# A spectral gate kernel: filtering the frequency columns in two passes, upper half first

## The chip, the core and the metric

The kernel runs on one core of one Trainium2 chip. The metric is device time in microseconds (us), the median of a few executions. A second number is the span of one profiled execution, from the first to the last of the program's own instructions; positions in the text ("at 72.1 us") count from the start of that span.

The core has a matrix engine (TensorE, PE in the profile, with its weight loads as PEld), a vector engine (VectorE, DVE), an activation engine (ScalarE, ACT), a general engine (GpSimd, POOL) and a queue engine that only issues transfers (SyncE, SP). Each runs its own list of instructions in order; semaphores make one engine wait for another.

## The reference, cut to what matters

```python
x = A_x                                       # (1, 2048, 1024) bf16
g = sigmoid((x * gate_w).sum(-1, keepdims=True))
def branch(x, w_r, w_i):                      # w: (2048, 513) bf16
    X = rfft2(x.astype(float32))              # over the 2048 rows and the 1024 columns
    return irfft2(X * (w_r + 1j * w_i), s=(2048, 1024)).astype(bf16)
out = g * branch(x, A_w_r, A_w_i) + (1 - g) * branch(x, B_w_r, B_w_i)
```

One forward transform of x, two products with filters of 513 frequency columns, two inverse transforms, and a mix of both by a gate of one number per row.

## The kernel before, in words

All transforms are matrix products with constant tables. The text names the steps as the code does:

- **s1**: eight groups of rows are loaded (`load.x`), folded (`fold`), multiplied on PE (`s1m`) and copied from the accumulators to the array FR by ACT or DVE (`s1e`). Together the sixteen `s1e` fill sixteen blocks of 1024 elements per partition, t = 0 to 15. Every later step needs all sixteen.
- **s2 and s4**: for each t the transform along the columns (`s2m`, copied by `s2e`) and the rest of the transform along the rows (`s4m`, copied by `s4e`). A block then holds real and imaginary parts in alternate partitions.
- **swap**: two transfers inside the on-chip memory that exchange even and odd partitions, so that a complex product needs no other partition.
- **xneg**: a change of sign in every second partition (on DVE or ACT), after the swap has read the block.
- **prod**: the product with the filters, both branches at once, on DVE. `prod2` takes the swapped block, `prod1` the signed one, each for one half h of the 512 frequency columns (h = 0 lower, h = 1 upper), 1024 elements per partition. That is 16 x 2 x 2 = 64 instructions. The results go to the array WP.
- **s5, s6, s7**: the inverse transform. `s5m.g`, g = 0 to 31, handles 16 columns (16 PE products, then the copy `s5e.g` by ACT or DVE); groups 0 to 15 are the lower half and 16 to 31 the upper. `s6m.p.h` and `s7m.i` follow; `s7c` (ACT) and `s7p` (DVE) take out the accumulators, `fin` (POOL and DVE) forms the output rows, `store` writes them.
- **the gate**: `gwm`, `gsm`, `stm`, `rowsum`, `zsm`, `zse` compute it; `zst` and `zld` send it through main memory to broadcast it, `rb` and `al` put it into the table of s6.
- **filters**: `load.W.b.f` brings block b (two values of t) of branch f into one of three buffers (`WR`), as whole rows of 513 columns: pieces of 2052 bytes.

The accumulators are four units of 1024 columns. A unit is taken by the next PE step in order and given back by the copy that reads it. The order on every engine is written out by hand in one list, `ORDER`; each entry is a step, its numbers and the engine or queue (a, d, p, s) that takes it. An entry's place in the list fixes its place on its engine and nothing else; the waits follow from the tiles that a step reads and writes:

```python
for job in ORDER.split():
    P.job = job
    name, *args = job.split(".")
    jobs[name](*(int(k) if k.isdigit() else k for k in args))
```

All instructions of one kind are issued by a helper, so a line of the profile is a kind: L309 transfers, L313 copies by ACT, L315 copies by DVE and POOL, L318 products on DVE, L322 and L324 `xneg` on ACT and DVE, L333 PE, L718 `s7p`, L724 `fin`.

Of the kernel before, what the change touches and what calls it, by code (L numbers as in the profile page):

```python
# [24 lines left out]
fold.6.0.d fold.7.0.d load.F2.s s1m.1.0 s1e.5.1.a s1e.1.1.a s1m.6.1 s1m.6.0 s1m.7.0 load.W.1.0.s load.CK.s s1e.6.1.d s1e.1.0.a s1e.6.0.a
s1m.7.1 s1e.7.0.a fold.2.0.d fold.2.1.d s1e.7.1.a s1m.2.0 s1m.2.1 s1e.2.1.a load.W.0.1.s s1e.2.0.d s2m.0 sig0 s2m.1 load.W.0.0.s s2e.1.d
gsm.0.4 s2e.0.a s4m.0 s4e.0.a s2m.2 gse.0.4.d s4m.1 s2m.3 s2e.2.d s4m.2 load.W.1.1.s w5.0.a swap.0.a s4e.1.a s4e.2.a load.W.2.1.s s2e.3.d
s2m.4 s2e.4.a s4m.3 s2m.5 prod2.0.0.d swap.1.s s4m.4 swap.2.s xneg.0.d gsm.4.4 prod2.0.1.d s4e.3.a s2m.6 load.W.2.0.s prod1.0.1.d s2e.5.a
s4e.4.a s4m.5 s2m.7 s2e.6.a prod1.0.0.d s4m.6 s4e.5.a prod2.1.0.d xneg.1.d swap.3.p prod2.1.1.d prod1.1.0.d prod1.1.1.d s2m.9 swap.4.s
prod2.2.1.d w5.1.a s2e.7.a prod2.2.0.d prod2.3.1.d w5.2.a xneg.2.d s4e.6.a xneg.3.a prod2.3.0.d s4m.7 load.W.3.0.s gse.4.4.a prod2.4.1.d  # L30
s4e.7.a s2e.9.a prod2.4.0.d load.W.3.1.s prod1.2.0.d gsm.8.4 swap.5.p swap.6.p prod1.2.1.d s2m.8 swap.7.s prod1.3.1.d prod1.3.0.d xneg.4.d
s2m.11 s2e.8.a s4m.9 prod2.5.1.d xneg.5.d s4m.8 prod1.4.1.d gse.8.4.a xneg.6.d prod1.4.0.d s2m.10 load.W.4.0.s s2e.11.a s4e.9.a load.W.4.1.s
s2m.12 prod2.6.0.d gsm.12.4 s4e.8.a s4m.11 s2e.10.a swap.9.p prod1.5.1.d s4m.10 prod2.5.0.d gse.12.4.a prod1.5.0.d s2m.13 w5.3.a xneg.7.a
s4e.11.a s4e.10.a swap.8.p prod1.6.0.d s2e.13.a prod2.6.1.d prod2.7.1.d load.W.5.0.s s2m.15 prod1.6.1.d s2m.14 xneg.8.d prod2.8.0.d
prod1.7.0.d s4m.13 w5.4.a load.W.5.1.s s2e.12.a xneg.9.a load.VC.s swap.11.p s4m.12 prod2.9.1.d s4e.13.a prod2.7.0.d prod2.9.0.d s2e.14.a
prod2.8.1.d w5.5.a prod1.7.1.d s4e.12.a prod1.9.0.d s4m.14 prod2.11.1.d swap.10.s swap.13.s prod1.8.0.d s2e.15.a prod1.9.1.d prod1.8.1.d stm
s4e.14.a s4m.15 xneg.11.a s4e.15.a load.W.6.0.s load.W.6.1.s xneg.10.a rowsum.0.d load.W.7.0.s prod2.10.1.d load.W.7.1.s prod1.11.1.d
xneg.13.a prod1.11.0.d swap.12.p xneg.12.a prod1.10.0.d swap.14.p prod2.13.1.d prod1.10.1.d w5.6.a swap.15.p prod1.13.1.d prod2.12.1.d
rowsum.1.d prod1.12.1.d rowsum.2.p xneg.14.a prod2.14.1.d xneg.15.a prod1.14.1.d zsm prod2.15.1.d prod1.15.1.d s5m.16 prod2.10.0.d ste.a
prod1.14.0.d w5.7.a s5m.24 s5m.26 zse prod2.11.0.d prod2.14.0.d stx.s prod1.15.0.d prod1.13.0.d prod1.12.0.d s5m.22 load.U5.s prod2.12.0.d  # L40
s5e.16.a s5m.23 s5e.24.a prod2.15.0.d s5e.22.a s5m.29 s5e.29.a zst.p s5m.27 s5e.23.a s5e.26.d prod2.13.0.d s5m.19 s5e.27.a s5m.30 s5m.25
s5m.6 s5e.30.a s5e.19.d s5e.6.a s5m.18 stp.2.d s5e.25.d s5m.3 s5e.18.a s5m.13 s5m.28 s5e.3.d stp.1.d s5e.13.a stp.0.d s5m.8 s5e.28.a s5e.8.d
s5m.31 s5m.15 s5m.17 s5e.31.a s5m.14 s5e.15.d s5m.10 s5e.17.a s5e.14.d s5e.10.a s5m.2 zld.s c0m rb.0.d s5m.21 c0e.d al.0.1.d s5e.2.a s5m.12
al.0.0.d load.DI.s s5m.1 s5e.21.a s5m.11 s5m.7 s5e.12.d s5e.1.a s5m.20 s5m.9 s5e.11.d s5m.5 s5e.7.a s5e.20.d s5m.0 s5e.9.a s5e.0.a s5m.4
# [8 lines left out]
fin.10.1.p s7p.11.1.d s6m.7.1 store.6.0.s fin.10.0.d store.1.0.s s7p.12.0.d store.8.1.s s6e.7.0.a s7p.12.1.d store.4.1.s store.7.1.s
store.9.0.s s6e.7.1.a fin.12.1.d fin.11.1.p store.3.1.s s7m.13 fin.12.0.p s7m.14 store.10.0.s s7c.13.a s7m.15 store.9.1.a s7c.14.a
s7p.13.0.d fin.11.0.p s7p.13.1.d s7p.14.0.d store.8.0.s store.12.0.a s7p.14.1.d s7c.15.a store.12.1.s store.10.1.s fin.13.0.d store.11.0.s
s7p.15.0.d store.14.0.s fin.13.1.p store.14.1.a s7p.15.1.d store.13.1.s store.11.1.a store.15.1.a store.15.0.s store.13.0.p
# [14 lines left out]
def make_consts():  # L71
# [187 lines left out]
def bass_gated_mix__spectral_gfnet__spectral_gfnet__prompt_kernel(nc, A_x, A_w_r, A_w_i, B_x, B_w_r, B_w_i, gate_w, out):  # L259
# [29 lines left out]
    def ps(col, dims):  # L289
        return AP(PS, col, [[4096, 128]] + [list(x) for x in dims])  # L290
# [510 lines left out]
```

## Time and profile before

| | |
|---|---|
| time, median of 3 runs | 133.83 us (133.65 to 135.38) |
| the profiled execution's own time | 134.36 us |
| its span | 132.1 us |
| busy: PE, DVE, ACT, POOL | 102.8, 106.5, 98.5, 40.3 us |
| bytes moved | 25.54 MB in 15602 packets |

A group's row of the profile gives the line, the engine, the operation, the tile written and the tile read with partitions and elements, the count, the busy time, the mean length of one in ns, and the idle time in front of them with what ended it. A row of a stretch gives, for each engine, busy time and count of instructions, then the granted clock of PE (1.00 is full speed), the mean busy share of the 16 transfer engines and the bytes moved per second. A row of the timeline gives start, length, engine, line, tiles and count. PEld overlaps PE. "SPq" is SP issuing a transfer.

### The profile page before, as it was taken

To read this page: it belongs to the slowest core of one execution; us is meant where nothing else is said; L and a number is where in the kernel's file an instruction comes from. 1 tells how busy PE (TensorE), PEld (TensorE's weight loads), DVE (VectorE), ACT (ScalarE), POOL (GpSimd) and SP (SyncE) were. 2 spreads that over 40 slices of the span, in tenths; PEclk is the share of its full clock that TensorE was granted. 3 is DMA by queue.
4 is the path that set the end of the run, shared out by engine and by line. 5 is a ranking of instruction groups with operands and counts; after the bars stand their busy time and mean duration, and the time that the engine had idled before them with its cause. 6 is when DMAs were issued, how large, how long until landed. Compare 5 with 4: busy or idle time off the path is not lost.

```text
span 132.1 us, 3396 instructions
## 1 busy us (share of the span) xinstructions
PE 102.8 (78%) x1383; PEld 82.6 (63%) x1383; DVE 106.5 (81%) x162; ACT 98.5 (75%) x132; POOL 40.3 (30%) x47
## 2 busy tenths in 40 slices
PE   6169899699999999542001999999999999999900
PEld 3047788566866576120001988999999999978400
DVE  0325677268999989999489997999799999999980
ACT  1603999948999999989852679999957998787310
POOL 3000000000315063025111000000004999999990
PEclk9999999999999999997555569999999999999995
DMA  4899999903579887877960946200000021335565
GB/s 109 240 360 344 349 393 377 353 21 119 188 269 268 294 294 250 323 240 245 330 249 10 321 158 211 117 5 0 5 0 5 0 97 66 135 143 204 201 235 205
DMA packets 15602, 25.54 MB, mean 193 GB/s; under 512 B 2514, under 2 KB 7394, under 8 KB 15330
## 3 DMA queue, kind: packets, MB, share of 16 engines
q1 hardware_dynamic: 12288, 20.31, 45.7%
q10 hardware_dynamic: 2306, 2.37, 5.4%
q0 software_dynamic: 992, 2.63, 5.1%
q8 instruction: 11, 0.18, 0.6%
q14 instruction: 5, 0.04, 0.1%
HBM read 16.90 MB, written 4.20 MB: 160 GB/s over the span
## 4 chain that ended last, share of the span: by engine, by line
PE 45%; DVE 15%; DMA 13%; ACT 8%; issue 7%; POOL 7%; SPq 2%; POOLq 0%; DVEq 0%; ACTq 0%
PE PS L333 45%; DVE WP L318 11%; POOL WR L724 7%; DMA WR<-in_B_w_i_dram 5%; ACT FR L313 5%; DMA WP<-c_E 4%; DMA FR<-FR 4%; ACT WP L313 3%; SPq L309 2%; DVE FR L718 2%; DVE FR L315 1%; ACT W L313 0%; DVE F L318 0%; POOLq L740 0%; POOL FR L309 0%
## 5 line engine op out<-in xcount | busy, mean ns | idle before, releaser
L313 ACT ACTIVATE FR<-PS 128x1024 bf16<-128x1024 f32 (+1 forms) x57 | 49.2, 908 | 16.9 <-PE PS L333 14.4
L318 DVE TENSOR_TENSOR WP<-FR,WR 128x1024 bf16<-128x1024 bf16 x64 | 39.9, 687 | 2.9 <-DMA WR<-in_B_w_i_dram 2.1
L313 ACT ACTIVATE WP<-PS 128x1024 bf16<-128x1024 f32 x35 | 34.0, 1025 | 5.7 <-PE PS L333 5.5
L724 POOL TENSOR_TENSOR WR<-FR 128x512 bf16<-128x512 f32 x18 | 26.8, 1516 | 29.8 <-DVE FR L718 29.7
L333 PE MATMUL PS<-FR,WP 128*128 128x128 bf16 (+2 forms) x384 | 32.1, 245 | 0.3 <-DVE FR L718 0.2
L333 PEld LDWEIGHTS PS<-FR,WP 128*128 128x128 bf16 x384 | 28.0, 130 | 3.9 <-DVE FR L718 0.9
L333 PE MATMUL PS<-CK,WP 128*128 128x64 bf16 x512 | 20.4, 207 | 3.5 <-DVE WP L318 2.9
L309 POOL DMA_DIRECT2D FR<-FR x18 | 9.9, 552 | 42.0 <-DVE WP L318 23.0
L333 PEld LDWEIGHTS PS<-CK,WP 128*128 128x128 bf16 x512 | 19.8, 120 | 3.9 <-DVE WP L318 3.0
L333 PE MATMUL PS<-FR,CK 128*128 128x512 bf16 x64 | 16.2, 380 | 3.3 <-ACT FR L313 3.2
L333 PE MATMUL PS<-WP 128*128 128x256 bf16 (+1 forms) x128 | 14.8, 281 | 4.4 <-DMA WP<-in_A_x_dram 3.3
L718 DVE TENSOR_TENSOR FR<-PS,FR 128x512 f32<-128x512 f32 x28 | 17.7, 678 | 0.3
L315 DVE CAST WP<-PS 128x1024 bf16<-128x1024 f32 (+1 forms) x14 | 15.9, 1166 | 2.1 <-PE PS L333 1.8
L333 PE MATMUL PS<-F,FR 128*128 128x256 bf16 x128 | 16.0, 273 | 1.5 <-ACT FR L313 1.2
L333 PEld LDWEIGHTS PS<-WP 128*128 128x128 bf16 x128 | 11.7, 108 | 8.1 <-DMA WP<-in_A_x_dram 4.1
L333 PEld LDWEIGHTS PS<-F,FR 128*128 128x128 bf16 x128 | 12.0, 98 | 5.3 <-ACT FR L313 1.8
L315 DVE CAST FR<-PS 128x1024 bf16<-128x1024 f32 x7 | 8.6, 1224 | 6.6 <-PE PS L333 6.6
L322 ACT ACTIVATE FR<-FR,SM 128x1024 bf16<-128x1024 bf16 x9 | 10.3, 1154 | 2.0 <-DMA FR<-FR 2.0
L333 PEld LDWEIGHTS PS<-FR,CK 128*128 128x128 bf16 x64 | 5.6, 98 | 9.2 <-ACT FR L313 4.7
L724 DVE TENSOR_TENSOR WR<-FR 128x512 bf16<-128x512 f32 x10 | 9.8, 981 | 0.1
L333 PE MATMUL PS<-ATB,CK 128*64 128x32 bf16 x1 | 0.2, 234 | 8.7 <-POOL ATB L315 8.7
L324 DVE TENSOR_SCALAR WP<-WP,SM 128x1280 bf16<-128x1280 bf16 (+1 forms) x3 | 1.4, 507 | 6.3 <-DMA SM<-c_SM 3.6
(44 smaller groups left out, 46.4 us busy)
## 6 DMA issues: line engine op xcount, KB each, us to landing
out_dram<-WR SPq DMA_DIRECT2D x24, 128.0 KB, 2.1
WP<-in_A_x_dram SPq DMA_DIRECT2D x11, 256.0 KB, 7.8
FR<-FR POOLq DMA_DIRECT2D x18, 128.0 KB, 4.1
WR<-in_A_w_r_dram SPq DMA_DIRECT2D x7, 256.5 KB, 3.6
WR<-in_A_w_i_dram SPq DMA_DIRECT2D x7, 256.5 KB, 4.5
WR<-in_B_w_r_dram SPq DMA_DIRECT2D x7, 256.5 KB, 5.1
WR<-in_B_w_i_dram SPq DMA_DIRECT2D x7, 256.5 KB, 5.8
FR<-FR SPq DMA_DIRECT2D x12, 128.0 KB, 2.6
```

What stands on the lines that cost most here:

```text
L309: return P.add(eng, lambda e: e.dma_start(dst, src), dma=name, **kw)
L313: P.add("act", lambda e: e.activation(dst, src, ACT.Copy), **kw)
L315: P.add(eng, lambda e: e.tensor_copy(dst, src), **kw)
L318: P.add(eng, lambda e: e.tensor_tensor(out=dst, in0=s0, in1=s1, op=ALU.mult), **kw)
L322: P.add("act", lambda e: e.activation(dst, src, ACT.Copy, scale=SM[:, col:col + 1]), **kw)
L324: P.add(eng, lambda e: e.tensor_scalar(out=dst, in0=src, scalar1=SM[:, col:col + 1], scalar2=None, op0=ALU.mult), **kw)
L333: P.add("pe", lambda e: e.matmul(o, lh, rh, start=first, stop=last), **kw)
L718: P.add(Q[eng], lambda e: e.tensor_tensor(out=o, in0=ps(u * 1024, [(1, 512)]), in1=eos(i), op=ALU.subtract if s else ALU.add), r=[("EO", i ...
L724: P.add(Q[eng], lambda e: e.tensor_tensor(out=od, in0=pv[:, :, 0, :], in1=pv[:, :, 1, :], op=ALU.subtract if s else ALU.add), r=[("PQ", i ...
```

## The change

The 512 frequency columns are now handled in two passes, h = 1 first.

- `s2m.p.h`, `s4m.p.h`, `swap.p.h` and `xneg.p.h` handle two values of t (p = 0 to 7) for one half of the columns. The elements per step stay at 1024. The `s2m` products have 128 columns in place of 256 and there are twice as many (256 for 128). For p = 0 `s4m` is cut in two, since t = 0 has tables of its own.
- `prod.t.h` does in one instruction of 2048 elements what `prod2.t.h` and `prod1.t.h` did in two of 1024: 32 instructions for 64. It needs the swap and the sign change both.
- The upper half's blocks lie in WP, in room that x and the table E have left; the lower half's stay in FR. No product of h = 0 may write before everything of h = 1 has been read.
- `load.W.h.b.m.f` brings half rows: pieces of 514 bytes (h = 1) or 512 bytes (h = 0), four values of t per block. A transfer of four rows moves half the bytes that one of two whole rows moved, so there are 72 transfers for 36.
- `s5m` of groups 16 to 31 stands between the lower half's steps.
- The first warm-up on PE has 14 products of 512 columns in place of 4. `sig0`, which loads the table of the sigmoid, stands ahead of the first `s1e`. The first group of rows is 5 in place of 4; 13 `s1e` are on ACT in place of 12.
- At the end DVE has 13 `fin` in place of 10 and POOL 15 in place of 18; `rb.0`, `rb.3` and three of the `al` move to POOL. The gate is loaded into F2, and U5, DI and the buffers of s7 get other places in FR.

```diff
-load.x.0.1.s warm.12x64x1.4x512x1 load.x.5.0.a load.GR.a load.x.5.1.a fold.4.0.d fold.3.0.d s1m.4.0 s1m.4.1 s1m.3.1 load.x.1.0.s fold.0.0.d
+warm.12x64x1.14x512x1 fold.7.0.d load.x.0.0.s s1m.5.0 load.x.0.1.s fold.0.1.d load.x.3.0.s fold.0.0.d load.x.3.1.s load.x.6.0.s egen.0.1
...
         elif what == "W":
-            b, f = k
...
-                    s = AP(src.tensor, src.offset + 2 * b * 513, [[32 * 513, 64], [(31 - 4 * b) * 513, 2], [1, 1026]])
-                    dma(Q[q], f"w{b}{f}", sl(WR, d0, [(1026, 2), (1, 1026)], p0=ri, np_=64, pstep=2), s, **kw)
...
+            h, b, m, f = k
+            slot, n = (4 * (1 - h) + b) % 3, 256 + h
...
+                    dma(Q[q], f"w{h}{b}{f}", sl(WR, slot * WS + (4 * j + 2 * f + pm) * RW, [(4 * RW, c), (1, n)], p0=ri, np_=64, pstep=2),
+                        AP(src.tensor, src.offset + row * 513 + 256 * h, [[32 * 513, 64], [st, c], [1, n]]), **kw)
...
+    U = [("prod", 0)]
+    def place(kind, p, h):
+        if h:
+            return WP, 8192 * (3 - kind) % 24576 + 1024 * p, [("U", kind, p)]
+        v = 2 * p + (kind == 1)
+        return FR, v * 1024, UK(v * 1024)
...
-    def xneg(t, eng):
-        sign(Q[eng], sl(FR, t * 1024, [(1, 1024)]), sl(FR, t * 1024, [(1, 1024)]), 1, r=["SM"], w=[("FR", t), ("XN", t)])
+    def xneg(p, h, eng):
+        T, o, K = place(1, p, h)
+        sign(Q[eng], sl(T, o, [(1, 1024)]), sl(T, o, [(1, 1024)]), 1, r=["SM"], w=K + [("XN", p, h)])
...
-        i0 = sl(FR, slot * 1024 + 256 * h, [(0, 2), (512, 2), (4, 64), (1, 4)])
-        o = sl(WP, h * HZ + (256 if k == 1 else 0) + 16 * t, [(8, 2), (4, 2), (BP, 64), (1, 4)])
+        i0 = sl(T, y + 512 * (t % 2), [(x - y, 2), (0, 2), (1, 512)]).rearrange("p k f (m q l) -> p k f m q l", m=2, l=4)
+        i1 = sl(WR, slot * WS + 4 * RW * (t % 4), [(0, 2), (2 * RW, 2), (RW, 2), (4, 64), (1, 4)])
+        o = sl(WP, h * HZ + 32 * t, [(16, 2), (8, 2), (4, 2), (BP, 64), (1, 4)])
```

What moves, on three engines. First PE, where the last steps of s2 and s4 meet s5. `PS<-F,FR` is `s2m`, `PS<-FR,CK` is `s4m`, `PS<-CK,WP` is `s5m` (16 per group), `PS<-GSB,CK` is `stm`, `PS<-ATB,CK` is `zsm`. Before:

```order
L333 MATMUL PS<-F,FR 128x256 x24
L333 MATMUL PS<-FR,CK 128x512 x12
L333 MATMUL PS<-GSB,CK 128x15 x2
L333 MATMUL PS<-GSB,CK 128x1 x2
L333 MATMUL PS<-FR,CK 128x512 x4
L333 MATMUL PS<-ATB,CK 64x32
L333 MATMUL PS<-CK,WP 128x64 x352
```

And now, at the same place:

```order
L333 MATMUL PS<-F,FR 128x128 x16
L333 MATMUL PS<-CK,WP 128x64 x16
L333 MATMUL PS<-GSB,CK 128x15 x2
L333 MATMUL PS<-GSB,CK 128x1 x2
L333 MATMUL PS<-CK,WP 128x64 x16
L333 MATMUL PS<-ATB,CK 64x32
L333 MATMUL PS<-CK,WP 128x64 x16
L333 MATMUL PS<-FR,CK 128x512 x8
L333 MATMUL PS<-CK,WP 128x64 x304
```

All of s5 stood behind the last `s4m`; now three groups of the upper half stand ahead of the last two `s4m`, and the other groups follow, upper half first.

Second ACT, around the last sign changes. `FR<-PS` with 1024 elements are `s4e` and `s2e`, `FR<-FR,SM` is `xneg`, `W<-WR` is `w5`, `WP<-PS 128x8x128` is `s5e`, `ZG<-PS` is `zse`, `XST<-PS` is `ste`. Before:

```order
L322 ACTIVATE FR<-FR,SM 128x1024
L313 ACTIVATE FR<-PS 128x1024
L322 ACTIVATE FR<-FR,SM 128x1024 x3
L313 ACTIVATE W<-WR 128x4 x2
L322 ACTIVATE FR<-FR,SM 128x1024 x2
L313 ACTIVATE XST<-PS 128x32
L313 ACTIVATE W<-WR 128x4 x2
L628 ACTIVATE ZG<-PS 64x32 x2
L313 ACTIVATE WP<-PS 128x8x128 x21
```

And now:

```order
L313 ACTIVATE WP<-PS 128x8x128 x2
L632 ACTIVATE ZG<-PS 64x32 x2
L322 ACTIVATE FR<-FR,SM 128x1024
L313 ACTIVATE FR<-PS 128x2x2x256 x2
L313 ACTIVATE WP<-PS 128x8x128 x3
L313 ACTIVATE XST<-PS 128x32
L313 ACTIVATE WP<-PS 128x8x128 x3
L322 ACTIVATE FR<-FR,SM 128x1024
L313 ACTIVATE WP<-PS 128x8x128
L322 ACTIVATE FR<-FR,SM 128x1024 x2
L313 ACTIVATE WP<-PS 128x8x128 x16
```

The last two `s4e` and the last four `xneg` of the lower half on ACT now stand between nine copies of the upper half's s5; the other sixteen copies follow.

Third SP, where filters are loaded into a buffer that is in use. The bracket names the semaphores that the transfer waits for (`d_w..` an earlier load, `s_dve` and `s_act` the products and `w5` that read it). Before, two blocks in a row:

```order
L309 DMA WR<-in_A_w_r_dram 64x2x1026 [waits d_w10,s_dve]
L309 DMA WR<-in_A_w_i_dram 64x2x1026
L309 DMA WR<-in_B_w_r_dram 64x2x1026 [waits d_w11]
L309 DMA WR<-in_B_w_i_dram 64x2x1026
L309 DMA WR<-in_A_w_r_dram 64x2x1026 [waits d_w20,s_dve]
```

And now, the first five of the eight transfers of one block:

```order
L309 DMA WR<-in_A_w_r_dram 64x4x256 [waits d_w120,s_dve,s_act]
L309 DMA WR<-in_A_w_i_dram 64x4x256
L309 DMA WR<-in_A_w_r_dram 64x4x256
L309 DMA WR<-in_A_w_i_dram 64x4x256
L309 DMA WR<-in_B_w_r_dram 64x4x256 [waits d_w121]
```

A block was four transfers for two values of t; it is eight for four values of t and half the columns.

More of the change, by code (lines that the diff above doesn't have):

```diff
@@ L25 @@
[L25 to L44, printed above, removed]
@@ L53 @@
[L53 to L56, printed above, removed]
+load.E.1.s load.SM.a load.x.5.1.a egen.1.3 load.x.5.0.s fold.5.0.d zero load.E.0.s egen.1.1 load.GR.a load.x.7.0.a egen.1.2 load.x.7.1.s
@@ L57 @@
+store.11.0.s s7c.14.a s7p.13.1.d s7c.15.a s7p.14.0.d s7p.14.1.d s7p.15.0.d s7p.15.1.d store.14.0.a store.14.1.a store.15.1.a fin.13.0.d
+fin.13.1.d store.15.0.s store.12.0.a store.13.0.s store.13.1.a store.12.1.p
 """
@@ L408, in load @@
         elif what == "VC":
[L409 removed]
+            dma(Q[q], "VC", sl(WP, VCo, [(1, 512)]).bitcast(u16), cst["V"].ap(), w=["VC"] + [("fold", FOLDED[0], k) for k in range(2)])
         elif what == "GR":
```

217 lines of the change are left out of this document (116 added, 101 removed).

## The prediction

> **What bounds the kernel now.** First the page's slices, where PE has a hole; then stretches cut at its edges, to see who works in it; then the chain, to see whether it sets the end.
>
> ```profile
> PE   6169899699999999542001999999999999999900
> PEclk9999999999999999997555569999999999999995
> 24.30:55.00 30.70, 30.23 (x312) 20.52 (x312) 26.32 (x44) 27.70 (x42) 6.66 (x12) 1.00 0.67 228
> 55.00:72.10 17.10, 2.39 (x13) 1.00 (x14) 14.52 (x25) 12.77 (x21) 4.46 (x8) 0.68 0.68 232
> 72.10:93.20 21.10, 20.57 (x528) 20.20 (x529) 19.40 (x27) 18.49 (x20) 0.00 (x0) 0.86 0.38 128
> 93.20:125.70 32.50, 32.14 (x390) 28.04 (x387) 31.77 (x46) 24.85 (x35) 24.75 (x18) 1.00 0.24 86
> ...
> 57.04 3.10 DVE WP L318 x5
> ...
> 62.77 6.64 DMA WR<-in_B_w_i_dram
> ...
> 69.54 2.52 DVE WP L318 x4
> 72.06 0.05 issue
> 72.10 5.32 PE PS L333 x96
> 77.42 0.02 issue
> 77.45 3.78 ACT WP L313 x4
> 81.23 0.05 issue
> 81.28 30.36 PE PS L333 x596
> ```
>
> From 55.0 to 72.1 PE works 2.39 of 17.1 us, and the clock falls. The chain there is products on DVE and a filter block; at 72.1 the first s5 group starts, when the last product of the upper half is done. Then come 21.1 us of s5 alone, and from 93.2 PE is full to the end. Two stages stand one behind the other that need not, as far as data goes: the last products and the first sixteen groups of s5.
>
> **The change, term by term.** I follow three queues to the start of s6 (93.2 before) and add the rest.
>
> ```profile
> 15.00:20.00 5.00, 4.59 (x53) 3.79 (x52) 4.30 (x7) 4.67 (x7) 0.00 (x0) 1.00 1.07 381
> 8.17 7.34 PE L333 MATMUL PS<-WP 128*128 128x256 bf16 x47 [0.69 <-DVE WP L315]
> L333 PE MATMUL PS<-F,FR 128*128 128x256 bf16 x128 | 16.0, 273 | 1.5 <-ACT FR L313 1.2 <-ACT GSB L313 0.2
> 17.48 6.76 ACT L313 ACTIVATE FR<-PS 128x1024 bf16<-128x1024 f32 x7 [0.33 <-PE PS L333]
> 31.67 0.68 DVE L318 TENSOR_TENSOR WP<-FR,WR 128x1024 bf16<-128x1024 bf16 x1
> FR<-FR SPq DMA_DIRECT2D x12, 128.0 KB, 2.6
> L324 DVE TENSOR_SCALAR FR<-FR,SM 128x1024 bf16<-128x1024 bf16 x7 | 3.4, 481 | 0.4 <-DMA FR<-FR 0.4
> ```
>
> *End of s1.* The first 47 wide products of s1 took 7.34 us, 0.156 each, where s2's of the same size take 16.0 / 128 = 0.125. A warm-up that lasts until they start saves at most 48 x 0.031 = 1.5 us of PE. The transfer engines are full (share 1.07), so the last rows arrive no earlier, about 18 us; one fold, 16 products and a copy behind them give 22. Between 22.0 and the 24.24 of before (17.48 + 6.76) I take 22.4, since the rows above show PE late in the first half.
>
> *First product.* Before it came 31.67 - 24.24 = 7.4 us later. Now three `s2m` of 1.1, an `s4m` of 0.9, a copy of 1.0, a swap of 2.6, then the sign change (0.40 start to start), which `prod2` didn't wait for: 8.3. So 30.7.
>
> ```profile
> L318 DVE TENSOR_TENSOR WP<-FR,WR 128x1024 bf16<-128x1024 bf16 x64 | 39.9, 687 | 2.9 <-DMA WR<-in_B_w_i_dram 2.1 <-ACT FR L322 0.5 <-DMA FR<-FR 0.3
> L318 DVE TENSOR_TENSOR PST<-XST,W 128x64 bf16<-128x64 bf16 x2 | 0.3, 184 | 0.0
> L718 DVE TENSOR_TENSOR FR<-PS,FR 128x512 f32<-128x512 f32 x28 | 17.7, 678 | 0.3
> 77.45 19.21 ACT L313 ACTIVATE WP<-PS 128x1024 bf16<-128x1024 f32 x20 [0.68 <-PE PS L333]
> 61.89 2.20 ACT L322 ACTIVATE FR<-FR,SM 128x1024 bf16<-128x1024 bf16 x2
> L313 ACT ACTIVATE W<-WR 128x4 bf16<-128x4 bf16 x16 | 2.4, 206 | 0.4 <-DMA WR<-in_B_w_i_dram 0.4
> 2.62 7.17 SPq L309 DMA_DIRECT2D WP<-in_A_x_dram  x10
> 19.14 0.61 SPq L309 DMA_DIRECT2D WR<-in_B_w_r_dram  x1
> 79.44 8.00 PE L333 MATMUL PS<-CK,WP 128*128 128x64 bf16 x224 [0.20 <-ACT WP L313]
> ```
>
> *DVE.* From 64 elements (184 ns) to 1024 (687) is 0.524 ns per element, so 2048 take 687 + 537 = 1224 ns. Successive ones overlap (39.9 / 64 = 0.62 for 687), so 1.15 each: 32 make 36.8 us, where 64 of 0.62 made 39.9. With eight sign changes (3.2) and the gate's two (1.3) DVE would be through at 30.7 + 41.3 = 72.0 if it never waited. It will, for two queues:
>
> *SP.* A transfer of this shape isn't in the trace. Its issue lies between 0.61 (filters, two rows) and 0.72 (x, four rows of 1 KB, 7.17 / 10); I take 0.66, nearer to the filters because x was issued into a filling queue. The lower half's block 0 needs the buffer that the upper half's eighth product releases, at about 42.8 (eight products, four sign changes and some 1.3 us of waiting for swaps). From there 12 + 8 + 8 + 8 = 36 issues of 0.66 and 2 us for a swap and a wait end at 68.6; with 2.7 to land (the swaps' 2.6) the last four products start at 71.3 and end at 75.9. A block takes SP 8 x 0.66 = 5.3 us and DVE 4 x 1.15 + 0.4 = 5.0, so SP is level with DVE the whole way: twice the transfers for the same bytes has used up its slack.
>
> *ACT.* Ahead of the first copy of s5 stand 28 copies of 0.96 (19.21 / 20), three sign changes of 1.10 and eight small ones of 0.2, 31.8 us; ACT idled 30.70 - 27.70 = 3.0 us in the corresponding stretch, mostly at its start, waiting for PE. So that copy starts at 57.2. To the last sign change of the lower half are nine copies of s5, two `s4e`, four sign changes and three small: 15.6, at 72.8. Behind it wait `prod.14.0`, `prod.15.0` and `prod.12.0`: 76.2. If ACT hadn't the upper half's copies ahead of that sign change it would be done 8.6 us earlier, and DVE or SP would set this point.
>
> Three ways, 72.0 unhindered and 75.9 and 76.2: I take 76.
>
> *Lower half of s5.* Sixteen groups at 8.00 / 14 = 0.57 and the extra one of 0.6 take PE to 85.8. ACT has 55 copies, seven sign changes and eleven small ones behind s1: 52.8 + 7.7 + 2.2 + 3.0 idle = 65.7, the last copy at 88.1; s6 may start two copies earlier, at 86.2. Both agree: **86.0** for 93.2.
>
> ```profile
> 93.22 24.32 PE L333 MATMUL PS<-FR,WP 128*128 128x128 bf16 x316
> 99.41 3.89 DVE L718 TENSOR_TENSOR FR<-PS,FR 128x512 f32<-128x512 f32 x6
> 112.94 1.71 DVE L724 TENSOR_TENSOR WR<-FR 128x512 bf16<-128x512 f32 x1
> L724 DVE TENSOR_TENSOR WR<-FR 128x512 bf16<-128x512 f32 x10 | 9.8, 981 | 0.1
> L724 POOL TENSOR_TENSOR WR<-FR 128x512 bf16<-128x512 f32 x18 | 26.8, 1516 | 29.8 <-DVE FR L718 29.7
> ```
>
> *The rest.* From s6 to the end were 132.1 - 93.2 = 38.9 us. PE's work is the same (32.14 busy of 32.50). DVE, at 31.77 of 32.50, gets three `fin` more at 0.98 (2.9 us), POOL three fewer at 1.5. Between nothing and 2.9 I take 2.0, nearer to the full price because DVE has 0.7 us to spare there. 86.0 + 40.9 = 126.9 of span. The profiled execution took 134.36 for 132.1, so 2.3 lie outside: 129.2; the median shown is 0.5 below that execution. Forecast **128.7**, 3.8% less.
>
> *Costed at nothing.* `s2m` in halves: 256 products at the 17.6 / 256 of s6's 128-wide ones are 17.6 for 16.0; PE has the hole for it. `rb.0` and two `al` on POOL: up to 3 + 1.5 + 1.5 us by its `fin`, behind the gate's landing near 70, beside the last products and the lower s5; uncovered they would cost up to 6. `sig0` leaves the end of s1 for its start, where ACT waits for rows anyway.
>
> **Rivals.**
>
> *The end gives it back* (0.15). DVE's `fin` take 0.68 alone and 1.71 beside POOL's; if half of thirteen do, the last stage grows by 6, not 2: 132.7. For it, DVE's 31.77 of 32.50; against it, POOL has fewer.
>
> *Issue binds the lower half* (0.10). At 0.72 per issue, 36 cost 2.2 us more, and a landing of 5.1, as the old filters' often was, 2.4: 133.3.
>
> ```profile
> 10.00:15.00 5.00, 5.00 (x37) 3.89 (x36) 2.56 (x5) 2.61 (x3) 0.29 (x1) 1.00 1.11 346
> WR<-in_B_w_r_dram SPq DMA_DIRECT2D x7, 256.5 KB, 5.1
> q1 hardware_dynamic: 12288, 20.31, 45.7%
> q10 hardware_dynamic: 2306, 2.37, 5.4%
> ```
>
> *Half rows cost as much as whole kilobytes* (0.09), **slower than before**. With 1 KB pieces the engines moved 346 GB/s. If a 514-byte piece takes as long, that is 173. The five loads ahead of the first product (2.6 MB behind the rows of x, from about 20) would land at 35, not 28, 4.5 us after DVE is ready; and a block of the lower half, 1.05 MB and two swaps, would take 7.6 us for DVE's 5.0. Together 11 us at the last product: 139.5. It decides where a piece takes more than about 30 ns: (5.0 us - 1.4 for the swaps) / 128 pieces per engine. Against it, a piece's time grows with its size: 0.457 x 16 x 132.1 / 12288 = 79 ns at a mean of 1653 bytes, 0.054 x 16 x 132.1 / 2306 = 49 ns at 1028; on that line 514 bytes take 25.
>
> The Trainium skill, "DMA: Bandwidth & Descriptors", section "Specifications", gives 512 bytes as the least for line rate, with a read-modify-write below it. The halves are 512 and 514 bytes, so by that rule the rival doesn't fire and the sum stands; the section "How a descriptor splits into AXI transactions" speaks against the change, since a piece that starts off a 256-byte boundary fetches bytes that aren't used, and rows of 1026 bytes start anywhere.
>
> *PE's clock halves while s5 trickles* (0.04). The upper half's groups come one per copy, 0.57 busy of 0.96. If the clock fell before the lower half, as after 55.0 (0.68 granted), its groups would take some 0.88, sixteen of them 5 us more: 133.7. Against it, PE was busy 2.39 of 17.1 when that happened. The Trainium skill, "TensorE: Matmul & The Clock Gate", section "A second HAM failure mode: psum-queue depth-cycling", tells of exactly such short gaps between groups, and by it this case would be likelier than I put it.
>
> *The wide product doesn't keep two elements per cycle* (0.02). `s7p`, with f32, takes 678 ns for 512; a rate of one would make 2.2 us of each and 33 us in all: 162.
>
> **How the numbers follow.** 0.60 for the forecast, 125 to 131. Two per cent, what a measurement here can tell, is 131.2 below and 136.5 above. Faster: 0.60 and a third of the first two rivals, 0.68. Same: the rest of these and the clock, 0.21. Slower: 0.11. The low end 124.5 is s1 at 22.0, ACT's idle 1 us shorter and the last stage unchanged; the high end 135.0 takes in the rivals up to 133.7. What is outside is 0.11 and a little of the forecast's own edge.
>
> **What would show it.** Right: no slice of PE below 3 between 55 and 72; `s5m` of the upper half from about 54; 32 products of some 1.2 us; the last near 76, released by an ACT sign change or a filter; s6 at 86; DVE full behind it. Wrong: the first product after 33 and released by filters (pieces too slow); DVE idle over 6 us between 30 and 76; a clock under 1 before s6; a last stage over 43 us. If ACT were through s5 much before 86, my sum of its queue is wrong, and I would be too slow.

## The result, and the profile after

The changed kernel takes **140.19 us** (median of 4 runs, 139.53 to 141.13) where the kernel before takes 134.05 in the same comparison: a ratio of 1.0445, 95% interval 1.0347 to 1.0542. The profiled execution took 139.92 for a span of 137.8, so again some 2.1 us lie outside the span. Here and below medians are of all runs of a kernel, while ratios leave out those that the comparison counts as disturbed (of twelve runs each, *Filters first* keeps three and *Two queues and that split* four).

The page's slices of the changed kernel, to be held against those of before:

```profile
PE   6859995999921999985885361999999979979900
PEclk9999999999996589999999555599999999999995
DMA packets 27890, 25.55 MB, mean 185 GB/s; under 512 B 3090, under 2 KB 23842, under 8 KB 27618
q1 hardware_dynamic: 24752, 19.92, 49.2%
```

The old hole of PE between 55 and 72 is gone, as intended: s5 of the upper half fills it. Others have come: two slices from 38 to 45, and one at 83 to 86. The stretches, cut at the first product, the last product of the upper half, the last product, the start of s6 and the end, show the same in each engine's busy time (PE, PEld, DVE, ACT, POOL):

```profile
24.30:35.59 11.29, 11.29 (x129) 8.36 (x127) 2.97 (x4) 9.89 (x12) 2.33 (x4) 1.00 0.75 200
35.59:60.53 24.94, 19.29 (x298) 14.51 (x294) 21.80 (x25) 17.32 (x26) 5.05 (x10) 0.86 0.66 190
60.53:85.62 25.09, 14.24 (x271) 11.43 (x269) 19.72 (x20) 22.75 (x27) 5.67 (x11) 0.82 0.87 261
85.62:96.62 11.00, 10.95 (x272) 10.86 (x273) 9.57 (x12) 7.92 (x9) 6.89 (x5) 0.80 0.16 63
96.62:137.80 41.18, 32.42 (x388) 28.03 (x384) 36.73 (x49) 26.11 (x36) 24.14 (x20) 0.96 0.28 103
```

So the first product starts at 35.6 (before: 31.67), the last one ends at 85.6, s6 starts at 96.6 (93.2), and the last stage takes 41.2 (38.9). Of the 5.7 us of span that were lost, 3.4 are ahead of s6 and 2.3 behind it.

Why the first product is late stands in SP's timeline (start, length, operation, tiles, how many in a row):

```profile
12.78 0.61 SPq L309 DMA_DIRECT2D WR<-in_A_w_r_dram  x1
...
15.51 1.90 SPq L309 DMA_DIRECT2D WR<-in_A_w_r_dram  x1
...
20.41 1.43 SPq L309 DMA_DIRECT2D WR<-in_A_w_r_dram  x1
...
31.64 0.63 SPq L309 DMA_DIRECT2D WR<-in_B_w_i_dram  x1
32.31 1.23 SPq L309 DMA_DIRECT2D WP<-WP  x2
...
34.22 0.65 SPq L309 DMA_DIRECT2D WR<-in_B_w_r_dram  x1
...
36.92 4.68 SPq L309 DMA_DIRECT2D WP<-WP  x6
...
46.38 0.62 SPq L309 DMA_DIRECT2D WR<-in_B_w_i_dram  x1
49.75 1.15 SPq L309 DMA_DIRECT2D FR<-FR  x2
51.00 0.65 SPq L309 DMA_DIRECT2D WR<-in_A_w_r_dram  x1
```

From 12.78 to 32.27 SP issues 24 filter transfers and nothing else, 0.81 us each: some take 0.61, others up to 1.90. Only then comes the first swap (`swap.1.1`), 4.8 us after ACT's copy that it reads was done (27.50). `swap.7.1` stands behind four more filters and goes out at 36.92; it lands 5.0 us later, where it took 3.0 in the kernel below that has the upper half on two queues. What waited for these two swaps, on DVE and on ACT, and then on PE:

```profile
35.07 0.49 DVE L324 TENSOR_SCALAR WP<-WP,SM 128x1024 bf16<-128x1024 bf16 x1 [5.63 <-DMA WP<-WP]
41.98 1.15 ACT L322 ACTIVATE WP<-WP,SM 128x1024 bf16<-128x1024 bf16 x1 [5.44 <-issue]
44.22 1.89 PE L333 MATMUL PS<-WP,CK 128*128 128x512 bf16 x4 [5.56 <-ACT WP L313]
```

ACT's sign change `xneg.7.1` (the page calls its idle time "issue", but the swap landed at 41.91, just ahead of it) holds up the copies behind it, and so PE. ACT's late copy `s4e.1.0` (48.70 to 49.73) then holds up SP: its swap at 49.75 stands ahead of the lower half's filters, whose buffer had been free since 46.9.

### The profile page after: what moved, and what is told of

It reads as the page before. It is cut to its first block, busy times and chain, and to the rows that moved or that the text cites. A ratio compares the mean times of both kernels' runs of the same rounds, so it can differ in the third digit from the quotient of the medians.

```text
span 137.8 us, 3668 instructions
## 1 busy us (share of the span) xinstructions
PE 107.4 (78%) x1529; PEld 87.5 (63%) x1529; DVE 101.7 (74%) x124; ACT 100.7 (73%) x124; POOL 45.4 (33%) x55
## 2 busy tenths in 40 slices
DMA packets 27890, 25.55 MB, mean 185 GB/s; under 512 B 3090, under 2 KB 23842, under 8 KB 27618
## 3 DMA queue, kind: packets, MB, share of 16 engines
q1 hardware_dynamic: 24752, 19.92, 49.2%
## 4 chain that ended last, share of the span: by engine, by line
PE 44%; ACT 16%; DMA 12%; DVE 10%; SPq 7%; issue 6%; ACTq 2%; DVEq 1%
PE PS L333 44%; ACT FR L313 11%; SPq L309 7%; DMA WR<-in_B_w_i_dram 6%; DVE WP L318 5%; DMA WP<-in_A_x_dram 5%; ACT WP L313 4%; ACTq L309 2%; DMA WP<-WP 2%; DVE FR L722 1%; DVE WR L722 1%; DVE WR L728 1%; ACT WP L322 1%; DVE WP L324 1%; DVEq L744 1%
## 5 line engine op out<-in xcount | busy, mean ns | idle before, releaser
L313 ACT ACTIVATE WP<-PS 128x1024 bf16<-128x1024 f32 x53 | 51.7, 1036 | 13.7 <-PE PS L333 13.6
L313 ACT ACTIVATE FR<-PS 128x1024 bf16<-128x1024 f32 (+1 forms) x44 | 36.2, 894 | 5.9 <-PE PS L333 3.5
L728 POOL TENSOR_TENSOR WR<-FR 128x512 bf16<-128x512 f32 x15 | 21.5, 1453 | 12.3 <-DVE FR L722 12.1
L318 DVE TENSOR_TENSOR WP<-FR,WR 128x2048 bf16<-128x2048 bf16 x16 | 18.7, 1222 | 5.4 <-DMA WR<-in_B_w_i_dram 5.4
L318 DVE TENSOR_TENSOR WP<-WP,WR 128x2048 bf16<-128x2048 bf16 x16 | 18.9, 1221 | 1.4 <-DMA WR<-in_B_w_i_dram 0.9
L333 PE MATMUL PS<-F,FR 128*128 128x128 bf16 x256 | 16.1, 221 | 1.2 <-ACT FR L313 1.2
L309 POOL DMA_DIRECT2D WP<-WP x8 | 4.5, 564 | 35.4 <-ACT WP L313 25.8
L728 DVE TENSOR_TENSOR WR<-FR 128x512 bf16<-128x512 f32 x13 | 13.8, 1094 | 0.0
L333 PE MATMUL PS<-WP,CK 128*128 128x512 bf16 (+4 forms) x44 | 9.1, 349 | 5.6 <-ACT WP L313 5.6
L309 POOL DMA_DIRECT2D FR<-FR x14 | 7.7, 554 | 13.1 <-PE PS L333 10.9
L318 POOL TENSOR_TENSOR FR<-FR,F 128x1024 bf16<-128x1024 bf16 x2 | 4.3, 2134 | 15.6 <-DMA F<-zd 15.6
```

The source lines that it names most:

```text
L309: return P.add(eng, lambda e: e.dma_start(dst, src), dma=name, **kw)
L313: P.add("act", lambda e: e.activation(dst, src, ACT.Copy), **kw)
L318: P.add(eng, lambda e: e.tensor_tensor(out=dst, in0=s0, in1=s1, op=ALU.mult), **kw)
L333: P.add("pe", lambda e: e.matmul(o, lh, rh, start=first, stop=last), **kw)
L728: P.add(Q[eng], lambda e: e.tensor_tensor(out=od, in0=pv[0], in1=pv[1], op=ALU.subtract if s else ALU.add), r=[("PQ", i % NPQ, 0), ("PQ", ...
```

## The experiments

The theories: **A**, SP's queue sets the time (72 filter issues, with swaps between them); **B**, the half rows load the transfer engines; **C**, the order of ACT's queue. The first four runs set A against the others, the next two ask which part of A, and the rest take the last stage, the start, and a version with the repairs. Positions in the profiled executions, in us:

| kernel | first product | `swap.7.1` landed | upper half's products end | last product ends | s6 starts | span | median |
|---|---|---|---|---|---|---|---|
| forecast | 30.7 | | | 76 | 86.0 | 126.9 | 128.7 |
| changed kernel | 35.6 | 41.9 | 60.5 | 85.6 | 96.6 | 137.8 | 140.19 |
| two queues, all | 31.6 | 36.6 | 53.8 | 77.2 | 88.1 | 130.3 | 134.11 |
| fewer issues | 35.4 | 36.1 | 57.9 | 81.6 | 93.0 | 134.2 | 136.20 |
| swaps off SP | 33.6 | 37.2 | 58.6 | 80.9 | 91.4 | 132.6 | 135.61 |
| two queues, upper half | 32.0 | 35.9 | 53.4 | 78.5 | 89.0 | 130.1 | 133.49 |
| two queues, lower half | 35.9 | 42.3 | 61.7 | 86.5 | 97.1 | 138.3 | 139.75 |

**Two queues, all.** Branch B's filters are issued by POOL; two of them move in the order so that POOL's queue takes them in turn, and the early ones wait for rows of x, so as not to come ahead of these.

```diff
-... load.W.1.1.1.1.s ... load.W.1.0.1.1.s ... load.W.1.2.1.1.s ... load.W.1.3.1.1.s ... load.W.0.0.1.1.s ...
+... load.W.1.1.1.1.p ... load.W.1.0.1.1.p ... load.W.1.2.1.1.p ... load.W.1.3.1.1.p ... load.W.0.0.1.1.p ...
```

> The changed kernel with branch B's half of the filter loads (36 of 72 transfers, same pieces, same bytes) issued from POOL's queue, the other half still from SP's; the first of them wait for rows of x that land near 16. Theory A (SP's queue is the bound: 72 issues of 0.66 us and the swaps stand one behind the other on it): the first swap is issued when its copy is done, about 27.5, the first product comes at 31 to 32 (35.6 in the changed kernel), the lower half's products are not released by filters, the last product at 77 to 80 (85.6), time 131 to 135. Theory B (half rows load the transfer engines themselves): bytes and pieces are the same, so the filters land as late as now, and the time stays at 139 to 141. Theory C (ACT's queue, in which sign changes stand behind copies of the upper half): the first product comes early, but the last not before 82, and the time is 136 to 138.

134.11 us (132.12 to 136.72, 10 runs), ratio to the kernel before 0.9955 (0.9894 to 1.0016). It was A's figure, and the last product at 77.2 is too early for C. First product, last product and s6 come within 0.9, 1.2 and 2.1 us of the forecast. Two things don't fit. A said that no product of the lower half would wait for filters, and two still do (1.72 us at 60.98, 1.13 at 72.05). And the pieces did not stay the same in the records: what POOL issues shows as fewer and larger packets (20786 in all for 27890), so this run alone does not put B aside.

**Fewer issues.** The first three blocks of the upper half in 12 transfers in place of 28, in the same pieces.

```diff
-... load.W.1.2.1.0.s load.W.1.1.1.0.s ... load.W.1.0.1.0.s ...
+... load.W.1.0.3.0.s ...
-... load.W.1.1.1.1.s ... load.W.1.0.1.1.s ... load.W.1.2.1.1.s ...
+... load.W.1.0.3.1.s ...
```

> The changed kernel with the first three blocks of the upper half loaded by 12 transfers (up to 12 rows each) in place of 28; the same pieces of 514 bytes, the same bytes, one more block ahead of the first product. The lower half's loads are as they were. Theory A: SP reaches the first swap near 25, so the first product comes at 31 to 32 and ACT no longer waits 5 us for the second swap; the lower half is still released by filters, so the last product gains 2 to 4 us: time 136 to 138. Theory B: the pieces land no earlier, the first product stays at 35 or later, the time at 139 to 141. Theory C: as A up to the first product, then no gain at all.

136.20 us (135.68 to 136.64), ratio 1.0201 (1.0118 to 1.0284): A's range, with as many pieces. But the issues did not become short. SP's timeline:

```profile
13.08 0.61 SPq L309 DMA_DIRECT2D WR<-in_A_w_r_dram  x1
13.73 2.04 SPq L309 DMA_DIRECT2D WR<-in_A_w_i_dram  x1
15.80 2.48 SPq L309 DMA_DIRECT2D WR<-in_A_w_r_dram  x1
18.32 3.33 SPq L309 DMA_DIRECT2D WR<-in_A_w_i_dram  x1
...
28.97 2.06 SPq L309 DMA_DIRECT2D WP<-WP  x2
```

Twelve issues take from 13.08 to 28.93, up to 3.33 us each: SP is held in the issue. Full transfer engines alone don't explain it. In the kernel before, SP's filter issues from 16 to 20 us took 0.61 each at a share of 1.05 to 1.08, and in *Filters first* those from 59.8 to 62.4 took 0.60 to 0.66 at 1.05. What differs early on is the number of pieces in a transfer: 128 before (64 partitions, two rows each), 256 in the changed kernel (up to 1.90 us), 704 in the transfer that took 3.33. No run changes that number alone, so this stays a reading. Two things then keep the first swap back, the count of issues and their length. The first product hardly moved (35.4, where A said 31 to 32: the swap's landing is still late, at 34.8), yet the upper half ends 2.7 us earlier. I read most of that as the price of the second swap's delay, since ACT no longer waits for it.

**Swaps off SP.** SP's five swaps on POOL's queue, which is idle then.

```diff
-swap.1.1.s  swap.7.1.s  swap.3.1.s  swap.5.1.s  swap.1.0.s
+swap.1.1.p  swap.7.1.p  swap.3.1.p  swap.5.1.p  swap.1.0.p
```

> The changed kernel with SP's five swaps issued from POOL's queue; all 72 filter transfers stay on SP. Theory A: the first swap is issued at 27.5 and ACT's wait of 5.4 us for the second one shrinks, but the filters ahead of the first product still land near 34, so it comes at 34 to 35; SP has ten issues less (6.5 us), the last product comes 2 to 4 us earlier and the time is 136 to 138. Theory B: 139 to 141. Theory C: 139 to 141, since ACT's order is the same.

135.61 us (2 runs, 134.75 and 136.48), ratio 1.0159 (1.0035 to 1.0283), a little better than A's range. The first swap lands at 32.1, and now the last filter (33.5) releases the first product. ACT waits 0.49 us in place of 5.44. No filter, no piece and no step of ACT was moved, so neither B nor C is needed for the 4.6 us that came back, of the 6.1 lost.

**The kernel before with twice the issues.** Each filter transfer as two of half the partitions: 72 for 36, in pieces of the same size.

```diff
+                for g in range(2):
+                    p0, off = ri + 64 * g, src.offset + 32 * g * 32 * 513
...
-                    s = AP(src.tensor, src.offset + 2 * b * 513, [[32 * 513, 64], [(31 - 4 * b) * 513, 2], [1, 1026]])
+                        s = AP(src.tensor, off + 2 * b * 513, [[32 * 513, 32], [(31 - 4 * b) * 513, 2], [1, 1026]])
```

> The kernel before with each filter transfer issued as two of half the partitions: 72 issues in place of 36, pieces and bytes unchanged. Theory A: SP then needs 8 x 0.65 = 5.2 us for the filters of eight products that take DVE 5.0, as in the changed kernel, so products are released by filters and the time rises to 137 to 142. Theory B (pieces, not issues): no change, 133.5 to 135. Theory C says nothing here: 133.5 to 135.

141.44 us (140.54 to 141.9, 4 runs), ratio 1.0587 (1.0509 to 1.0665). It is A's range, 7.7 us above the kernel before. But the edit changed more than the count: a piece of 2052 bytes took a median of 122 ns, where it took 85 in the kernel before, and the transfer engines were busier for no more bytes (the same stretch of the kernel before, shown in the prediction, ends in 0.67 and 228):

```profile
24.30:55.00 30.70, 27.65 (x299) 19.51 (x300) 23.25 (x38) 25.36 (x38) 6.59 (x12) 1.00 0.83 223
```

So the 7.7 us are not the price of the count alone, and this run puts B aside no more than the first one does. *Swaps off SP* does so for most of the loss, and so does the next pair. No run has small pieces at an unchanged count, so a smaller share of B is not measured by itself.

**Which half.** Branch B's filters of one half alone on POOL's queue: 18 of that half's 36 transfers (the recorded text says 16 of 32; block 0 has six per branch, not four).

```diff
-... load.W.1.1.1.1.s ... load.W.1.0.1.1.s ... load.W.1.2.1.1.s ... load.W.1.3.1.1.s ...
+... load.W.1.1.1.1.p ... load.W.1.0.1.1.p ... load.W.1.2.1.1.p ... load.W.1.3.1.1.p ...
```

> The changed kernel with 16 of the upper half's 32 filter transfers (branch B's) issued by POOL; the lower half's 36 stay on SP. Theory A1 (the loss is in the upper half: 24 issues ahead of the first swap, 8 ahead of swap 7, and the lower half only inherits the delay): first product near 31.6 as with all of branch B on POOL, the lower half's first filters issued near 44 in place of 51.0, and from there the 34.6 us to the last product that the changed kernel shows, so last product near 79, s6 near 90, time 133.5 to 135.5. Theory A2 (the lower half's 36 issues on one queue are the bound by themselves): the last product stays within 2 us of 85.6, time 138 to 140. Theory B (the half rows load the transfer engines): as many pieces, so 139 to 140.

133.49 us (132.29 to 136.09, 10 runs), ratio 0.9961 (0.9921 to 1.0): the whole gain of the first experiment, at the lower edge of A1's range. Its stretches, cut at the same five events:

```profile
24.30:31.97 7.67, 7.67 (x99) 6.16 (x97) 3.08 (x4) 6.26 (x8) 3.20 (x6) 1.00 0.92 249
31.97:53.43 21.46, 21.33 (x329) 15.94 (x326) 21.46 (x25) 20.75 (x30) 9.05 (x17) 1.00 0.73 226
53.43:78.47 25.04, 15.55 (x269) 11.83 (x269) 19.64 (x20) 22.69 (x27) 5.30 (x11) 0.79 0.86 264
78.47:88.99 10.52, 10.47 (x273) 10.39 (x273) 9.16 (x12) 7.92 (x9) 6.93 (x5) 0.85 0.15 62
88.99:130.10 41.11, 32.42 (x388) 28.03 (x384) 36.77 (x49) 26.13 (x36) 24.17 (x20) 0.95 0.28 103
```

In the upper half DVE is busy for all of 21.46 us and PE for 21.33 at full clock; in the changed kernel they are busy 21.80 and 19.29 of 24.94. The lower half's stretch, with all 36 transfers on SP, is as long as it was: 25.04 for 25.09. It is only earlier. The counterpart moves the lower half's:

```diff
-... load.W.0.0.1.1.s ... load.W.0.1.1.1.s ... load.W.0.2.1.1.s ... load.W.0.3.1.1.s ...
+... load.W.0.0.1.1.p ... load.W.0.1.1.1.p ... load.W.0.2.1.1.p ... load.W.0.3.1.1.p ...
```

> The changed kernel with 16 of the lower half's 32 filter transfers (branch B's) issued by POOL; the upper half's stay on SP. Theory A1: the first product stays at 35.6 and DVE leaves the upper half at 60.5; with both queues moved the lower half's products took 23.0 us against 23.6, so little is won: 138 to 139.5. Theory A2: the last product comes 6 to 8 us earlier, time 132 to 134. Theory B: 139 to 140.

139.75 us (139.06 to 140.43, 4 runs), ratio 1.0465 (1.0395 to 1.0534): no gain, against A2; it is a little above A1's range and within B's. Against B stands the pair: both kernels have the same 24338 packets, and only the one that clears SP in the upper half is faster. The two queues together take the lower half from 25.1 to 24.7 us.

**Filters first.** On two queues, POOL's filters for the lower half ahead of swaps that wait for ACT, and the last two swaps on SP.

```diff
-... load.W.0.1.1.0.s s2m.6.0 swap.3.0.p ... load.W.0.1.1.1.p swap.4.0.p stm load.W.0.2.1.0.s ... load.W.0.2.1.1.p ... swap.6.0.p ... swap.7.0.p
+... load.W.0.1.1.0.s load.W.0.1.1.1.p s2m.6.0 swap.3.0.p ... stm load.W.0.2.1.0.s load.W.0.2.1.1.p swap.4.0.p ... swap.6.0.s ... swap.7.0.s
```

> The changed kernel with branch B's filters on POOL's queue, as in the first of these runs (134.1), and besides: on POOL the filters of the lower half's second and third block ahead of the swaps that wait for ACT, and the last two swaps on SP behind its last filters. Theory A: those filters go out at 51 and 54.5 in place of 54.2 and 57.8, so the wait of 1.7 us before the lower half's fourth step goes, and the last swap's 7.2 us behind the filters shorten: last product near 74.5, s6 near 86, 131 to 132.5. If ACT's copies are the bound by then, or the transfer engines are full from 52 to 72 whatever the order: 133.5 to 134.5.

134.79 us (132.54 to 135.32, 12 runs) beside 134.04 for the kernel before, ratio 0.9916 (0.9846 to 0.9986). So no gain over 134.11. The filters went out nearly as early as expected (51.7 and 55.9, for 51 and 54.5), and the wait went to another transfer. One stretch and one row of DVE:

```profile
54.65:66.00 11.35, 8.12 (x113) 5.76 (x111) 8.18 (x9) 8.59 (x12) 8.93 (x16) 0.74 1.01 298
64.06 0.49 DVE L324 TENSOR_SCALAR FR<-FR,SM 128x1024 bf16<-128x1024 bf16 x1 [3.17 <-DMA FR<-FR]
```

The transfer engines are full there (share 1.01), and a swap issued behind the filters at 58.35 lands at 64.03. With the issues out of the way the lower half is held by the transfer engines. They moved 298 GB/s here, where the kernel before had 381 at a share of 1.07, so the small pieces have a part in it as well as the bytes.

**The last stage: fewer on DVE.** Three `fin` given back to POOL, as in the split of before.

```diff
-fin.2.1.d  fin.5.1.d  fin.10.1.d
+fin.2.1.p  fin.5.1.p  fin.10.1.p
```

> The changed kernel with three of the thirteen last steps on DVE given back to POOL, the split of the kernel before (10 and 18). If DVE's extra steps made the last stage 41.2 in place of 38.9, it is near 39.5 again: time 138 to 138.9, DVE no longer busy for all of 106 to 126. If the last stage is longer for another reason (the order of the last steps, the stores), 139.7 to 140.5.

140.75 us (138.45 to 141.41, 4 runs), ratio 1.0439 (1.033 to 1.0547): no gain that shows. It is worth a look at the groups of DVE's `fin`, first of the changed kernel, then of this one:

```profile
L728 DVE TENSOR_TENSOR WR<-FR 128x512 bf16<-128x512 f32 x13 | 13.8, 1094 | 0.0
```

```profile
L728 DVE TENSOR_TENSOR WR<-FR 128x512 bf16<-128x512 f32 x10 | 14.1, 1429 | 0.0
```

Ten take as long as thirteen did. The timeline of this run, DVE's row and POOL's beside it:

```profile
124.78 4.37 DVE L728 TENSOR_TENSOR WR<-FR 128x512 bf16<-128x512 f32 x1
123.63 4.97 POOL L728 TENSOR_TENSOR WR<-FR 128x512 bf16<-128x512 f32 x4
```

One `fin` of DVE, 0.68 us when alone, lasts 4.37 while POOL runs four of its own, and DVE's next step waits behind it. What counts is where the two engines' steps meet, not how many DVE has.

**Two queues and that split.** The first kernel of this section with the same three `fin` on POOL.

> The changed kernel with branch B's filter transfers on POOL's queue (all 36) and the split of the last steps as before (10 on DVE, 18 on POOL). The first edit alone gave 134.1. Theory A and the price of the last steps add: 132 to 133, 1 to 2 per cent below before. If POOL's steps, which now stand behind its own filter issues, come late, or if the last stage is bound by DVE's other work: 134.

133.65 us (131.47 to 139.03, 12 runs) beside 133.98, ratio 0.9883 (0.9827 to 0.994). The spread is wide, and its profile has the same ten `fin` at 1421 ns, so I read no gain of the split from it.

**The last stage in the old order.** From s6 on, the kernel before's entries of `ORDER`, apart from those already done.

```diff
-s6m.1.1 s6m.0.1 s6m.0.0 rb.3.p s6e.0.1.d ... fin.13.0.d fin.13.1.d store.15.0.s ... store.12.1.p
+s6m.1.1 al.1.0.d al.1.1.d s6m.0.1 s6e.1.1.a ... rb.3.d ... store.15.1.a store.15.0.s store.13.0.p
```

> The changed kernel up to the first step of s6, and from there the kernel before's order of steps (10 last steps on DVE and 18 on POOL, in the old places; alphas on DVE and ACT). If it is the order in which DVE's and POOL's last steps meet that made the last stage 41.2, it is 38.9 to 39.5 again and DVE's last steps cost 1.0 us each: time 138 to 138.5. If the last stage is longer because of what stands ahead of it (rb and al late, the s5 copies of the end): 139.5 to 140.5.

137.9 us (136.44 to 138.28, 4 runs), ratio 1.0249 (1.0184 to 1.0315). The last stage and the group of `fin` (its line is numbered six higher here):

```profile
95.56:134.30 38.74, 31.55 (x380) 27.62 (x379) 32.99 (x48) 25.18 (x36) 27.92 (x20) 0.98 0.30 110
L734 DVE TENSOR_TENSOR WR<-FR 128x512 bf16<-128x512 f32 x10 | 9.9, 988 | 0.1
```

38.7 for 41.2, and DVE's steps cost 0.99 again. DVE has ten `fin` and POOL eighteen, as in *fewer on DVE*, so their number is not what differs. The old order also gives other `fin` to each engine, and moves a copy of `s7c`, `rb.3`, two `al` and some stores; which of these counts, no run separates.

**Both repairs.** The upper half's filters on two queues, and the old order from s6 on.

> Both repairs: half of the upper half's filter transfers issued by POOL (alone: 133.5) and from s6 on the order of the kernel before. If the two add: 131 to 132, 1.5 to 2 per cent below the kernel before. If the last stage is not shortened by its old order: 133.5.

**131.63 us** (130.47 to 132.71, 6 runs) beside 134.16 for the kernel before, ratio **0.9762** (0.9698 to 0.9826). The two add, and this version is faster than both kernels, than the one before by 1.7 to 3.0 per cent.

**The warm-up alone.** The kernel before with 14 wide products in its warm-up for 4.

```diff
-warm.12x64x1.4x512x1
+warm.12x64x1.14x512x1
```

> The kernel before with only the warm-up lengthened (4 to 14 wide products), all else as it was. If the colder clock on the first products of s1 is what the longer warm-up removes, the first 47 wide products take about 0.13 each in place of 0.156, s1 ends 0.5 to 1.5 us earlier and the time falls by at most that: 132.5 to 133.7. If the rows of x, which come no earlier, set the end of s1 anyway: no change, 133.8, s1's last copy at 24.2.

133.9 us (132.44 to 140.76, 10 runs), ratio 0.9989 (0.9947 to 1.0031). Its timeline on PE and ACT:

```profile
8.97 1.92 PE L333 MATMUL PS<-WP 128*128 128x256 bf16 x16 [0.90 <-DVE WP L315]
16.95 6.76 ACT L313 ACTIVATE FR<-PS 128x1024 bf16<-128x1024 f32 x7 [0.65 <-PE PS L333]
```

The first products of s1 do take 0.12 us in place of 0.156, and ACT ends s1 at 23.7, 0.5 earlier. The first product of the filters comes 0.5 earlier too (31.14), and s6 starts at 92.91 for 93.22. What is left is too little for the medians to tell.

## Why the prediction was wrong, step by step

The span came out 10.9 us above the 126.9 that I had worked out: 4.9 at the first product, 3.3 from there to the lower half's first filters, 1.4 in the lower half, 1.0 in the rest of s5 and 0.3 in the last stage.

*End of s1*: right, 22.66 for 22.4.

*First product*: **the step that failed**, 35.6 for 30.7. "copy 1.0, swap 2.6" let the swap start when its copy was done (27.50 here, near my own chain). I had counted the filters ahead of it as bytes, in a rival, and not as issues on the queue that the swap shares. At my own 0.66 the 24 issues from 12.78 would have ended at 28.6, 1.1 us after the copy; that they took 0.81 each added another 3.7 us. So the missing sum of the queue is the smaller part of the 4.8 us and the price of an issue the larger. The row of 1.90 above and the 3.33 of the merged transfers are this. The change puts swaps behind filters on SP; I added up that queue for the lower half and not for the upper. The sign was there: "first product after 33 and released by filters (pieces too slow)". DVE waited for the swap, and the swap for the issuing of filters, so the cause I gave in brackets was not it; small pieces may have their part through the length of an issue. The filters themselves were next: with the swaps off SP the last of them landed at 33.5, and the first product was still 2.9 us late.

*SP*, "lower half's block 0 at 42.8": 51.0, 8.2 late, the first product's 4.9 and 3.3 more. This second piece is the same queue again: `swap.7.1` behind filters, ACT 5.44 us idle, `s4e.1.0` late, and SP's own swap ahead of the filters waiting for it. With the upper half on two queues that issue falls at 43.9, 1.1 off the forecast.

*SP*, "SP is level with DVE the whole way": near enough. From there to the last product were 34.6 us for my 33.2. The issue mostly took 0.60 to 0.68 (I had 0.66). The landings behind the last issue of a block were larger than my 2.7; the chain shows two:

```profile
65.59 3.82 DMA WR<-in_B_w_i_dram
...
76.92 3.94 DMA WR<-in_B_w_i_dram
```

So *Issue binds the lower half* had the sign right, since filters released the products of each block. But half of that half's transfers on another queue gained nothing (139.75), so the issues are not its only bound; with both halves on two queues the transfer engines are full there (1.01 above). The Trainium skill, "DMA: Bandwidth & Descriptors", section "Issuing engines are not separate DMA queues", says that starting transfers on several engines saves only the sequencer's time, "which is usually small relative to the DMA itself". In the lower half the runs agree; in the upper half they don't: there the second queue was worth 6.7 us (140.19 to 133.49), because swaps stood behind it.

*DVE*: the price was right, 1222 ns for 1224:

```profile
L318 DVE TENSOR_TENSOR WP<-WP,WR 128x2048 bf16<-128x2048 bf16 x16 | 18.9, 1221 | 1.4 <-DMA WR<-in_B_w_i_dram 0.9 <-ACT WP L322 0.5
L318 DVE TENSOR_TENSOR WP<-FR,WR 128x2048 bf16<-128x2048 bf16 x16 | 18.7, 1222 | 5.4 <-DMA WR<-in_B_w_i_dram 5.4
```

From the first product to the last DVE is busy 41.5 of 50.0 us, so its idle time passes the 6 us that I named as a sign.

*ACT*: 76.2 from the sum of its queue was too early by the idle time in it: I allowed 3.0 us, and `xneg.7.1` alone cost 5.44.

*Lower half of s5*: 11.0 us from the last product to s6 for my 10.0. The rival of PE's clock happened here in part: 0.82 while the groups come in drops, 0.80 behind it. The first six groups after the last product against the last ten:

```profile
85.67 4.99 PE L333 MATMUL PS<-CK,WP 128*128 128x64 bf16 x96 [4.15 <-DVE WP L318]
...
91.04 5.69 PE L333 MATMUL PS<-CK,WP 128*128 128x64 bf16 x160
```

0.83 us each, then 0.57; six groups, not sixteen, pay for it.

*The rest*: 41.2 for 40.9. The sum was right by luck, **its reason wrong**. "Three more `fin` on DVE" is not what costs: ten took 14.1 us where thirteen took 13.8, and in the old order ten took 9.9 and the stage 38.7. *The end gives it back* named the right mechanism, DVE's step beside POOL's; the stage grew by 2.3 us for its 6.

*Half rows cost as much as whole kilobytes*: gave nearly the time that was measured, 139.5, for a reason that the runs speak against. 24752 packets of a mean of 805 bytes took 0.492 x 16 x 137.8 us, 43.8 ns each, where the line of the prediction gives 38; the trace's records of the 514-byte pieces alone have a median of 28 ns and a mean of 34, about the 30 from which I said that it decides. A byte did cost more in them: 514 bytes in 28 ns are 18 per ns, 2052 in 85 before were 24. So it was nearer than I thought. But the merged transfers were 4.0 us faster with the same pieces, the swaps off SP 4.6, and the first stretch after the first product has a share of only 0.66. Where pieces and bytes do bind is the lower half, once the issues are out of the way (1.01 above).

*Costed at nothing*: the `s2m` halves and `sig0` were covered. `rb.0` came at 85.84, not near 70, since the transfers that bring the gate back stood behind the filters on SP (79.49); the last of them, at 96.04, was still ahead of s6.

## What to carry to other kernels

When a change multiplies the transfers on a queue, add up that queue in time order like an engine, with every small transfer that something waits for, and ask of each what stands ahead of it; the bytes may fit and the issues too, and a swap of 2.6 us still come 5 us late. Bulk loads and urgent exchanges belong on different queues, above all where the issuing itself is held. And when two engines slow each other in a stage, compare the mean length of a step by its place: moving steps from one to the other can leave the sum where it was.

## What the runs showed of the hardware

- An issue on SP is not a fixed price: mostly 0.60 to 0.68 us, but up to 1.90 in the changed kernel and 3.33 for merged transfers, and it holds all that stands behind it. Full transfer engines alone did not lengthen it (0.61 before, at a share of 1.05 to 1.08). With the upper half on two queues, POOL's issues from 16.2 to 22.4 us took 0.54 to 0.78 each, while those that SP began from 17 to 21 took 0.97 to 2.03.
- The same pieces of 2052 bytes took a median of 122 ns each in transfers to 32 partitions and 85 in transfers to 64 (the kernel before with twice the issues, and the kernel before).
- A `fin` on DVE (two operands in on-chip memory) waits out several of POOL's in a row, 4.37 us for 0.68. The Trainium skill, "SBUF — State Buffer", section "SBUF: two separate sides", describes an exclusive lock on a port pair between the two, held for the length of an instruction. This fits the trace as far as the two exclude each other; but DVE's instruction, once waiting, was passed by three further ones of POOL that started behind it.
